# A fused attention and feed-forward block: four early copies placed on other engines

## The chip, the cores and the metric

The kernel runs on one core of a Trainium2 chip. A core has a matrix engine (TensorE, PE in the profile, with its weight loads listed apart as PEld), three engines for elementwise work (VectorE or DVE, ScalarE or ACT, GpSimd or POOL), and SyncE (SP), which here only issues DMAs. Each engine works through its own list of instructions in order; between engines the order is kept by semaphores. The metric is the device time of one execution in microseconds (us). Several runs are given by their median, lowest and highest.

## The reference

All inputs are bfloat16. S is 2048 tokens, D 448, H 16 heads of Dh 28, the attention window W 256, F 1792.

```python
xn = _layernorm(x, axis=-1)                       # (x - mean) / sqrt(var + 1e-5)
return x + _A_ref(xn, A_wqkv, A_wo) + _B_ref(xn, B_w_gate, B_w_up, B_w_down)
...
qkv = (lambda x, *d: x.transpose(*d))((x @ wqkv).reshape(B, S, 3, H, Dh), 2, 0, 3, 1, 4)
scores = jnp.einsum("bhqd,bhkd->bhqk", q, k) * (Dh ** -0.5)
mask = (idx[:, None] - idx[None, :] >= 0) & (idx[:, None] - idx[None, :] < W)
scores = jnp.where(mask[None, None], scores, -1e9)
p = _softmax(scores, axis=-1)
o = jnp.einsum("bhqk,bhkd->bhqd", p, v)           # then @ wo
...
return (_gelu(x @ w_gate) * (x @ w_up)) @ w_down  # B
```

Both branches read the same normalized rows; their sum and x give the output.

## The kernel before

The 2048 rows are 16 tiles of 128. Four tiles make a block of 512 query columns (`qb` 0 to 3). A block runs through attention (scores, exponentials, masks, products with v) and then through the gated feed-forward; while the scores of a block are at work, matmuls of other stages are fed in between by a planner with costs in ns (`Feed`, `share`). The change lies ahead of all this, in the straight prologue of lines 674 to 720, which is written out by hand: each engine's list is in the order of the calls there. The prologue normalizes the first four tiles, turns them and makes the q, k and v of the first block for the first group of four heads.

One tile `t` goes through these steps. `stat(t)` (lines 195 and 196, DVE) takes mean and variance of 448 columns. `rstd(t)` (lines 200 and 201, ACT) makes 1/sqrt as exp of a logarithm. `norm(t)` (line 209) writes `xn`, 512 columns: 448 normalized ones by DVE (the main part), and then the last 64 a second time into columns 448 to 511 (the doubled columns). The doubling exists because 448 is three and a half times 128: the fourth chunk of 128 rows holds the same 64 rows twice, so that two half-height matmuls can use both halves of the array. For tiles 1, 2, 5, 6 and 7 the doubled columns are written by POOL, for all others by DVE. `xn` has four buffers. `transp(t)` (lines 223 and 224) turns the four chunks on PE into PSUM, chunk 3 being the one with the doubled columns, and one engine copies the result to `xnT`. `v_dense` and `proj` (line 228) are the three full chunks of a projection, `v_half` and `qk_halves` (line 234) the half-height rest.

The weights also need a layout of their own. Heads of 28 are padded to 32 columns, so `pads` (line 665) copies raw q or k columns from `wraw` to `wqp` or `wkp`, group by group of four heads, and line 692 does the same for the last 64 weight rows of q and of k, into `w3p`: on partitions 0 to 63 those of q, on 64 to 127 those of k. `proj(pq, wqp, 0, 0)` needs the first group of `wqp`, the `proj` for k needs `wkp`, and `qk_halves` needs `w3p`. After `norm(3)` comes `make_masks` on POOL: one memset of 768 columns (line 155) and 18 small selects (line 161).

SP issues the loads of x and the weights in the order of the listing. ACT issues those of x tile 1 and of the first q and k columns ahead of its own work. None of these issues is in the part that changes.

Of the kernel before, what the change touches and what calls it, by code (L numbers as in the profile page):

```python
# [15 lines left out]
S, D, H, Dh, F = 2048, 448, 16, 28, 1792  # L16
# [59 lines left out]
def kernel(  # L76
# [11 lines left out]
    nc = tc.nc  # L88
# [25 lines left out]
    wraw = blk.tile([P, 4, 2 * D], bf16, name="wraw", tag="hT")  # L114
# [54 lines left out]
    wqp = const.tile([P, 3, H, 32], bf16, name="wqp")  # L169
    wkp = const.tile([P, 3, H, 32], bf16, name="wkp")  # L170
    w3p = const.tile([P, H, 32], bf16, name="w3p")
# [33 lines left out]
    def norm(t):  # L205
        xn = work.tile([P, 4, P], bf16, name="xn", bufs=4)
        xf = xn[:, :, :].rearrange("p a b -> p (a b)")
        for eng, lo, n, src in ((nc.vector, 0, D, 0), (nc.gpsimd if t in (1, 2, 5, 6, 7) else nc.vector, D, 64, 384)):
            eng.tensor_scalar(out=xf[:, lo:lo + n], in0=x_sb[:, t, src:src + n], scalar1=mv_all[:, t, 0:1],
                              scalar2=rstd_all[:, t:t + 1], op0=ALU.subtract, op1=ALU.mult)  # L210
        xns[t] = xn
# [5 lines left out]
    def transp(t, n, copy, tag):  # L217

        tp = psum.tile([P, 2, 4, P], bf16, name="tp", tag=tag, bufs=2 if tag == "m" else 1)
        for i in range(n):  # L220
            xn = xns.pop(t + i)
            for c in range(4):
                nc.tensor.transpose(out=tp[:, i, c, :], in_=xn[:, c, :], identity=ident[:, :])
        copy(out=xnT[:, :, t * P:(t + n) * P].rearrange("p c (i q) -> p i c q", q=P), in_=tp[:, 0:n, :, :])
# [15 lines left out]
    def bank(name):  # L240

        tag = ring[0][ring[1] % len(ring[0])]
        ring[1] += 1
        return psum.tile([P, QB], f32, name=name, tag=tag, bufs=2 if tag == "m" else 1)


    def v_dense(t, pv):
        mm3(pv, lambda c: xnT[:, c, t * P:(t + 1) * P], lambda c: wv[:, c, :], True, False)
# [411 lines left out]
    def pads(eng, dst, gs):  # L660

        hs = slice(4 * gs.start, 4 * gs.stop)
        c0 = D * (dst is wkp)
        src = wraw[:, 0:3, c0 + Dh * hs.start:c0 + Dh * hs.stop]
        eng(out=dst[:, :, hs, 0:Dh], in_=src.rearrange("p c (h d) -> p c h d", d=Dh))
# [11 lines left out]
    stat(1)  # L677
    rstd(1, 1)
    norm(0)
    transp(0, 1, nc.scalar.copy, "o")  # L680
    stat(2)
    norm(1)
    rstd(2, 1)
    warmup(1)
# [3 lines left out]
    pvs = [bank("pv")[:, 0:D]]  # L688
    v_dense(0, pvs[0])
    norm(2)  # L690
    pads(nc.vector.tensor_copy, wqp, slice(0, 1))
    nc.vector.tensor_copy(out=w3p[:, :, 0:Dh], in_=wraw[:, 3, 0:D].rearrange("p (h d) -> p h d", d=Dh))
    pads(nc.scalar.copy, wkp, slice(0, 1))
    transp(2, 1, nc.scalar.copy, "o")
    pvs.append(bank("pv")[:, 0:D])
    v_dense(1, pvs[1])
    norm(3)
# [246 lines left out]
```

## Time and profile before

| | us |
|---|---|
| median of 3 runs | 221.85 |
| lowest, highest | 221.24, 221.89 |
| the profiled execution's own time | 221.75 |
| its span, first to last instruction | 220.0 |
| outside the span | 1.75 |
| PE busy in the span | 213.2 (97%) |
| DVE, ACT, POOL busy | 153.1, 133.3, 48.0 |

The table holds one profiled execution beside three unprofiled ones. All times inside the span are counted from its first instruction. In the timeline view a line gives the start, the duration, the engine, the line of the kernel, the operation, its output and inputs with their shapes, the count (several instructions of one kind are merged, and the duration is then that of the whole stretch), and in brackets how long the engine was idle before and what ended that. [...] In the view of the chain that ended last a line has a start, a length, an engine, an output and a line of the kernel. The PE is busy without a gap from 20 to 60 us; the prologue is the stretch up to about 12 us.

### The profile page before, as it was taken

The numbers are of one execution on the slowest core, as the hardware profiler recorded it, in microseconds if no ns is written. First come the engines' busy times: TensorE is split into PE (matmuls) and PEld (weight loads), VectorE is DVE, ScalarE is ACT, GpSimd is POOL, SyncE is SP. The second block draws the span as 40 slices with busy tenths as digits, with TensorE's granted clock in tenths as the row PEclk, the third lists the DMA queues.
The fourth block names the chain that finished last, engine by engine and source line by source line (L and its number), as shares of the span: only waits on it lengthen the run. The fifth ranks groups of instructions, "written<-read, shape, count | busy, mean of one in ns | idle before, by whom it ended". The sixth has DMA issues, their size and how long they took to land.

```text
span 220.0 us, 5437 instructions
## 1 busy us (share of the span) xinstructions
PE 213.2 (97%) x2281; PEld 95.8 (44%) x2281; DVE 153.1 (70%) x346; ACT 133.3 (61%) x131; POOL 48.0 (22%) x81
## 2 busy tenths in 40 slices
PE   6999999999999999999999999999999999999992
PEld 2433333444444454444444445444344445434571
DVE  5987896799666883669566795385345898579422
ACT  3588788662878875432878887233576777574000
POOL 5767987320000220022000021022000022022000
PEclk9999999999999999999999999999999999999999
DMA  6996799203200001101400000200000000000010
GB/s 188 308 293 89 188 316 289 56 1 75 45 3 21 24 24 28 19 11 38 71 1 24 24 0 24 53 12 0 0 3 21 25 3 24 24 1 0 22 46 25
DMA packets 18045, 13.30 MB, mean 60 GB/s; under 512 B 8704, under 2 KB 16992, under 8 KB 18016
## 3 DMA queue, kind: packets, MB, share of 16 engines
q1 hardware_dynamic: 17072, 12.62, 22.3%
q8 instruction: 19, 0.31, 0.6%
q10 hardware_dynamic: 944, 0.29, 0.5%
q14 instruction: 10, 0.08, 0.1%
HBM read 9.15 MB, written 2.18 MB: 51 GB/s over the span
## 4 chain that ended last, share of the span: by engine, by line
PE 93%; DVE 3%; DMA 1%; ACT 1%; issue 0%; DVEq 0%
PE po L376 20%; PE gt L228 16%; PE u L228 12%; PE sc L611 6%; PE po L371 6%; PE gt L234 5%; PE ue L228 5%; PE ov L571 5%; PE pq L228 4%; PE pv L228 4%; PE pk L228 3%; PE pq L234 1%; PE g L228 1%; DMA x_sb<-in_A_x_dram 1%; PE ue L234 1%; PE pv L234 1%
## 5 line engine op out<-in xcount | busy, mean ns | idle before, releaser
L617 ACT ACTIVATE p_sb<-sc 128x2048 bf16<-128x2048 f32 (+2 forms) x42 | 73.8, 1757 | 12.6 <-PE sc L611 8.2
L376 PE MATMUL po<-wd,hT 128*128 128x448 bf16 (+1 forms) x238 | 49.8, 342 | 0.0
L459 ACT ACTIVATE ge<-gt 128x1024 bf16<-128x1024 f32 x26 | 26.6, 1024 | 34.9 <-PE u L234 20.1
L537 POOL TENSOR_TENSOR oN<-oc,l 128x512 bf16<-128x512 f32 x12 | 16.0, 1332 | 137.8 <-DVE l L551 87.4
L228 PE MATMUL gt<-xnT,wg 128*128 128x512 bf16 x156 | 37.5, 380 | 0.0
L466 DVE TENSOR_TENSOR hT<-ge,u 128x512 bf16<-128x512 bf16 x40 | 25.7, 682 | 12.9 <-ACT ge L459 12.9
L376 PEld LDWEIGHTS <-hT 128*128 128x128 bf16 x238 | 21.5, 98 | 18.8 <-issue 2.6
L228 PE MATMUL u<-xnT,wu 128*128 128x512 bf16 x120 | 29.2, 379 | 0.0
L518 DVE TENSOR_TENSOR p_sb<-p_sb,masks 128x256 bf16<-128x256 bf16 (+1 forms) x90 | 26.8, 352 | 0.4 <-ACT p_sb L617 0.4
L228 PEld LDWEIGHTS <-wg 128*128 128x128 bf16 x168 | 15.3, 98 | 21.3 <-issue 4.5
L228 PEld LDWEIGHTS <-wu 128*128 128x128 bf16 x168 | 16.0, 98 | 19.2 <-issue 1.0
L556 DVE TENSOR_TENSOR oc<-oc,ov 128x512 f32<-128x512 f32 x12 | 8.2, 686 | 16.5 <-ACT oc L555 16.5
L611 PE MATMUL sc<-qT,kT 28*64 28x320 bf16 (+7 forms) x640 | 16.9, 263 | 0.2
L410 DVE CAST hT<-ue 128x512 bf16<-128x512 f32 x16 | 10.2, 681 | 8.3 <-PE ue L234 8.3
L371 PE MATMUL po<-wo,oN 128*128 128x448 bf16 (+1 forms) x68 | 15.9, 343 | 0.0
L381 DVE TENSOR_TENSOR res<-po,x_sb 128x448 bf16<-128x448 f32 (+1 forms) x17 | 9.9, 585 | 8.6 <-PE po L376 8.4
L528 POOL TENSOR_SCALAR_AFFINE_SELECT p_sb<-p_sb 128x512 bf16<-128x512 bf16 (+1 forms) x20 | 14.2, 729 | 5.4 <-ACT p_sb L617 5.4
L234 PE MATMUL gt<-xnT,wgu 64*128 64x512 bf16 (+1 forms) x67 | 12.7, 380 | 0.0
L555 ACT COPY oc<-ov 128x512 f32<-128x512 f32 x12 | 7.0, 583 | 8.8 <-PE ov L571 8.8
L228 PE MATMUL pq<-xnT,wqp 128*128 128x512 bf16 x45 | 12.2, 380 | 0.1
L543 DVE STREAM_TRANSPOSE l<-oc 128x512 f32<-128x512 f32 x16 | 11.3, 703 | 1.4 <-POOL oN L537 1.2
L228 PE MATMUL ue<-xnT,wu 128*128 128x512 bf16 x48 | 12.0, 380 | 0.0
(92 smaller groups left out, 243.4 us busy)
## 6 DMA issues: line engine op xcount, KB each, us to landing
out_dram<-res SPq DMA_DIRECT2D x15, 112.0 KB
x_sb<-in_A_x_dram SPq DMA_DIRECT2D x3, 448.0 KB
wu<-in_B_w_up_dram SPq DMA_DIRECT2D x1, 1344.0 KB
wg<-in_B_w_gate_dram SPq DMA_DIRECT2D x1, 1344.0 KB
wd<-in_B_w_down_dram SPq DMA_DIRECT2D x3, 448.0 KB
wraw<-in_A_wqkv_dram SPq DMA_DIRECT2D x2, 252.0 KB
wo<-in_A_wo_dram SPq DMA_DIRECT2D x4, 98.0 KB
wv<-in_A_wqkv_dram SPq DMA_DIRECT2D x1, 336.0 KB
```

The lines of the kernel that those rows point to most:

```text
L228: nc.tensor.matmul(ps, lhsT=lhs(c), rhs=rhs(c), start=start and c == 0, stop=stop and c == 2, skip_group_check=True)
L234: nc.tensor.matmul(ps[c:c + m], lhsT=lhs[p0:p0 + 64, c:c + m], rhs=rhs[p0:p0 + 64], start=start, stop=stop, tile_position=(p0, c), skip_gr ...
L371: nc.tensor.matmul(po[:, 0:w], lhsT=oN[:, g, cs], rhs=wo[:, g, lo:up], start=(g == 0), stop=False, skip_group_check=True)
L376: nc.tensor.matmul(po[:, 0:w], lhsT=hT[:, f, cs], rhs=wd[:, f, lo:up], start=False, stop=(f == NF - 1), skip_group_check=True)
L459: nc.scalar.activation(out=ge[:, :, :], in_=pr["gt"][:, :, :], func=ACT.Gelu_apprx_tanh)
L466: nc.vector.tensor_tensor(out=hT[:, f + i, :], in0=ge[:, i, :], in1=u, op=ALU.mult)
L518: nc.vector.tensor_tensor(out=reg, in0=reg, in1=m, op=ALU.mult)
L528: nc.gpsimd.affine_select(out=reg, in_=reg, pattern=mid + [[1 if diag else -1, min(w, P)]], compare_op=ALU.is_ge, fill=0.0, base=0 if diag ...
L537: nc.gpsimd.tensor_tensor(out=oN[:, g, :], in0=oc[:, :], in1=inv, op=ALU.mult)
L543: nc.vector.transpose(out=l1[:, :, :].rearrange("p a b -> p (a b)"), in_=oc[:, :])
L611: nc.tensor.matmul(ss[k0:k0 + nk, j, col:col + nq], lhsT=kT[r, g, kt * P + k0:kt * P + k0 + nk], rhs=qT[r, g, qb * QB + q0:qb * QB + q0 + ...
L617: nc.scalar.activation(out=p_sb[:, :, 0:ncol], in_=ss[:, :, 0:ncol], func=ACT.Exp, scale=SCALE)
```

## The change

Four pieces of work move to another place; nothing is computed in another way. The doubled columns of tile 0 go from DVE to POOL. The first group of `wqp` is copied by ACT and not by DVE, and the copy of `w3p` by POOL and not by DVE. On ACT, the copy of tile 2's turned chunks out of PSUM now comes ahead of the two padding copies.

```diff
     def norm(t):
         xn = work.tile([P, 4, P], bf16, name="xn", bufs=4)
         xf = xn[:, :, :].rearrange("p a b -> p (a b)")
-        for eng, lo, n, src in ((nc.vector, 0, D, 0), (nc.gpsimd if t in (1, 2, 5, 6, 7) else nc.vector, D, 64, 384)):
+        for eng, lo, n, src in ((nc.vector, 0, D, 0), (nc.gpsimd if t in (0, 1, 2, 5, 6, 7) else nc.vector, D, 64, 384)):
...
     pvs = [bank("pv")[:, 0:D]]
     v_dense(0, pvs[0])
     norm(2)
-    pads(nc.vector.tensor_copy, wqp, slice(0, 1))
-    nc.vector.tensor_copy(out=w3p[:, :, 0:Dh], in_=wraw[:, 3, 0:D].rearrange("p (h d) -> p h d", d=Dh))
-    pads(nc.scalar.copy, wkp, slice(0, 1))
     transp(2, 1, nc.scalar.copy, "o")
+    for dst in (wqp, wkp):
+        pads(nc.scalar.copy, dst, slice(0, 1))
+    nc.gpsimd.tensor_copy(out=w3p[:, :, 0:Dh], in_=wraw[:, 3, 0:D].rearrange("p (h d) -> p h d", d=Dh))
     pvs.append(bank("pv")[:, 0:D])
     v_dense(1, pvs[1])
     norm(3)
```

The lists of PE and SP keep their order. DVE's list loses three instructions. ACT's list gains the `wqp` copy and has, after the logarithm and exponential of tile 3, the copy of tile 2, then `wqp`, then `wkp`. POOL's list has, after its two opening memsets of `v_sb` (lines 142 and 143), the doubled columns of tiles 0, 1 and 2, then `w3p`, then the masks. Three waits are new: chunk 3 of tile 0 on PE waits for POOL, the weight loads of the first q projection wait for ACT and those of `w3p` for POOL; and `norm(4)` on DVE, which writes the `xn` buffer that tile 0 had, now also waits for POOL.

## The prediction

> **What bounds the kernel.** I read the page first: the shares of the engines and the chain that ended last.
>
> ```profile
> PE 213.2 (97%) x2281; PEld 95.8 (44%) x2281; DVE 153.1 (70%) x346; ACT 133.3 (61%) x131; POOL 48.0 (22%) x81
> ...
> PE 93%; DVE 3%; DMA 1%; ACT 1%; issue 0%; DVEq 0%
> ```
>
> 93% of the chain is PE. The change touches no matmul, so it can only move the moment from which PE has work without a break; later stages move along with it. The 3% of DVE lie in the prologue, as the chain of 4 to 14 us shows:
>
> ```profile
> 7.51 0.31 DVE wqp L665
> 7.82 0.87 DVE w3p L692
> 8.69 0.32 DVE xn L209
> 9.01 0.05 issue
> 9.05 0.44 PE tp L223 x4
> 9.49 0.57 PE pv L228 x3
> 10.06 1.40 PE s L228 x6
> ```
>
> Two of the copies that leave DVE are on it, ahead of tile 3's normalization. So the gain cannot be the 0.31 + 0.87 by itself: it is what tile 3's chain wins until its next limit. For that, the timelines of DVE, POOL and ACT, 7 to 9.7 us:
>
> ```profile
> 7.23 0.36 DVE L209 TENSOR_SCALAR xn<-x_sb,mv_all,rstd_all 128x448 bf16<-128x448 bf16 x1
> 7.51 0.31 DVE L665 COPY wqp<-wraw 128x336 bf16<-128x336 bf16 x1
> 7.74 0.94 DVE L692 COPY w3p<-wraw 128x448 bf16<-128x448 bf16 x1
> 8.61 0.60 DVE L209 TENSOR_SCALAR xn<-x_sb,mv_all,rstd_all 128x448 bf16<-128x448 bf16 x2
> 9.53 0.42 DVE L224 COPY xnT<-tp 128x512 bf16<-128x512 bf16 x1 [0.33 <-PE tp L223]
> ```
>
> ```profile
> 7.21 0.68 POOL L209 TENSOR_SCALAR xn<-x_sb,mv_all,rstd_all 128x64 bf16<-128x64 bf16 x1 [0.92 <-ACT rstd_all L201]
> 7.82 0.73 POOL L155 MEMSET masks<- 128x768 bf16 x1
> 8.63 1.29 POOL L161 TENSOR_SCALAR_AFFINE_SELECT masks<-masks 64x64 bf16<-64x64 bf16 x5
> ```
>
> ```profile
> 7.27 0.58 ACT L224 COPY xnT<-tp 128x512 bf16<-128x512 bf16 x1 [0.16 <-PE tp L223]
> 7.75 0.30 ACT L200 ACTIVATE lnv<-mv_all,eps_t 128x1 f32<-128x1 f32 x1
> 8.08 0.20 ACT L201 ACTIVATE rstd_all<-lnv 128x1 f32<-128x1 f32 x1
> 8.19 0.45 ACT L665 COPY wkp<-wraw 128x336 bf16<-128x336 bf16 x1
> 8.55 0.58 ACT L224 COPY xnT<-tp 128x512 bf16<-128x512 bf16 x1
> ```
>
> To see: the exponential that gives tile 3's scale ends at 8.28, DVE starts tile 3 at 8.61 only because the w3p copy is in front. That copy took 0.94 for 448 columns, where the wqp copy of 336 took 0.31; it lies beside POOL's memset of the masks.
>
> **The change, part by part.**
>
> *Tile 0's doubled columns, DVE to POOL.* DVE starts its next work 0.21 earlier (5.24 to 5.45). POOL is idle from 3.64 and starts 0.11 after the scale, as it did for tile 1 (5.60 to 5.71): 4.87 + 0.11 = 4.98. Its five such instructions last 0.57 to 0.68, so it ends at 5.55 to 5.66, against 5.54 on DVE. Chunk 3 of tile 0 is late by 0 to 0.1; I take 0.05, the mean of the ends. ACT's copy of tile 0 (6.09), tile 2's logarithm and exponential (6.58, 6.91) follow it: tile 2's scale comes at 7.16, not 7.11. POOL's pad of tile 1 starts at 5.71 as before.
>
> *What the 0.21 is worth.* Statistics of tile 2 and the main part of tile 1 are 0.21 earlier, so tile 1's chunks are turned at about 6.4 and not 6.62. ACT's copy of tile 1 waited 0.16 for that and now waits for ACT's own exponential of tile 2: about 7.07, not 7.27. Logarithm and exponential of tile 3 follow: its scale at 8.08, not 8.28. Tile 2 gains nothing: its scale is 0.05 later, and so are POOL's pad (7.94) and chunk 3 of its turn.
>
> *The two copies off DVE.* Tile 3 now starts when its scale is there: 8.08 + 0.09 = 8.17 instead of 8.61. Undisturbed, its two parts (0.60) are done at 8.77 instead of 9.21.
>
> *ACT's order.* The copy of tile 2 no longer waits for wkp: it starts when tile 2 is turned, 8.33 + 0.02 = 8.35, and ends at 8.93 instead of 9.13. wqp then takes 8.83 to 9.28 and wkp 9.19 to 9.64 (0.45 each by the wkp row). They are needed by the q projection (10.01 before) and the k projection (10.65 before): hidden. If tile 3 were 0.7 earlier still, wqp would be next.
>
> *PE.* The v matmuls of tile 1 end issuing at 8.73; tile 3's first chunks can go then (before: 9.05), chunk 3 at 8.94, v of tile 2 at 9.01 (its copy is there at 8.93), DVE's copy of tile 3 at 9.21 and the q projection at 9.69 instead of 10.01. Sum if POOL disturbs nothing: **-0.32**.
>
> *w3p on POOL.* It starts behind tile 2's pad, at 7.87. POOL copies no such shape before. Lower bound: its small copies (line 321, 48 columns, 0.16 from start to start) and their slope against 16 columns (0.14) give 0.4; upper bound: the strided memset of v_sb, 768 columns, 1.53. Nearest in size is the select of 512 columns, 0.63; I take 0.55. It is needed at 11.39 by the half-height matmuls: it would have to last 3 us to be late. Behind it the masks end at 14.1 (15.1 at the bound) instead of 13.57; POOL's next work started at 15.11, on an exponential of ACT. Hidden.
>
> *What tile 3 meets on DVE.* The memset of the masks goes from 7.82 to about 8.42, beside tile 3. The only row that shows a DVE copy beside that memset is w3p itself: 0.94, and 0.31 + 112 columns at the 0.35 ns that the larger pads show would be 0.35; so 0.59 was lost to it. Bounds of what it costs tile 3: nothing (main parts at 7.23, 17.36 and 18.36, beside POOL's pads and selects, keep 0.36), or 0.59. The memset falls behind the main part (8.17 to 8.53) and ahead of the doubled columns (8.45), as it fell behind wqp and ahead of w3p; by that nearest row I take 0.4 to 0.59 on the doubled columns. They end at about 9.3, and the q projection is at 10.1: -0.32 + 0.4 (the PE slack is used first) gives **+0.1**.
>
> [...]
>
> *New waits.* norm(4) at 14.04 waits on POOL for tile 0's pad, done at about 5.6: nothing; behind it would be DVE's v and kT casts and the transposing DMA of tile 4 on SP. The DMA queues get no new work, and no DMA wait stands in this stretch behind 3.47, so the loads hide nothing here.
>
> The sum is against the profiled 221.75 (220.0 + 1.75), which is 0.10 under the median: 221.75 + 0.1 = **221.85**. A measurement of this kernel tells about 0.3% (0.67) from no change.
>
> **The rivals.**
>
> 1. *Undisturbed tile 3.* The memset costs DVE nothing: -0.32, 221.4. For it: the three unlengthened main parts. Against: the w3p row.
> 2. *Both parts of tile 3 blocked.* POOL's w3p copy also holds DVE's main part, from 8.17 to the copy's end (8.42), and the memset then takes its 0.59: tile 3 ends at 9.6, and the cost is 9.6 - 9.21 = +0.4, 222.15. For it: the same w3p row; against: 17.36. [...]
> 3. *Slower: the clock step of PE moves.* The first v product of 448 columns is followed after 0.38, the next after 0.35, the third after 0.19: PE runs at half rate until about 7.75, and the eight warm-up matmuls before took 0.45 each, not 0.215. The work from 7.75 to the end of the q and k projections at 11.3 is seven v products, eight turns and six projections: 7 x 0.19 + 8 x 0.065 + 6 x 0.215 = 3.1 us. At half rate each us of later step costs up to 0.9; some slack (0.3) goes first. A step late by 1.7 costs about 1.2, 222.95; from about 1.1 on it is over 0.3%. For it: tile 0's chunk 3 now waits for POOL, and the spread of the runs, 0.65, fits a step that wanders. Against: PE's other gaps get smaller. [...]
> 4. *Faster by more.* -0.32, and the step comes earlier by the 0.35 that the first two v products lose: -0.7, 221.05. Against: tile 2's turn waits for POOL's pad at 7.94, whatever PE's rate.
>
> **How the numbers follow.** Forecast (doubled columns blocked, +0.1): 0.36. Rival 1: 0.24, of which 0.05 end under -0.3% by the spread of the runs. Rival 2: 0.12, of which 0.04 end over +0.3%. Rival 3: 0.17. Rival 4: 0.11. Faster: 0.05 + 0.11 = 0.16; slower: 0.04 + 0.17 = 0.21; within: 0.63. The range goes from 221.1 (rival 4 mostly left out) to 222.9 (the dearer half of rival 3 left out). The likeliest case's own range, from the bounds of the block, is 221.5 to 222.2.
>
> **What would show it.** Right: ACT's copy of tile 2 ahead of 8.4, tile 3's main part at about 8.2, its doubled columns ending at 9.1 to 9.4, the q projection at 9.9 to 10.2, w3p on POOL under 0.8, and the same PE busy time after 20 us. Doubled columns at 8.8 would be rival 1, a main part of 0.6 rival 2; v products of 0.35 after 8 us rival 3. I would be wrong with a wait that I count as hidden (w3p at 11.4, the masks at 15.1), or if a shift of some tenths changes the order in which exponentials and matmuls meet in the first block, where DVE is busy 4.91 of 5 us from 15 to 20.

## The result, and the profile after

| | median, us | lowest to highest | runs |
|---|---|---|---|
| before | 221.50 | 221.12 to 221.89 | 22 |
| after | 221.81 | 221.43 to 222.29 | 22 |

The changed kernel takes 1.0017 times as long, with a 95% interval of 1.0011 to 1.0023: slower by about 0.4 us (0.3 by the medians). The three runs that the prediction started from have a median of 221.85; more runs of the same kernel put it at 221.50. So the predicted 221.85 lies next to the measured 221.81, but the predicted step (+0.1, no change) does not: there is a loss, clear of the noise. That the two levels agree is luck: the profiled 221.75 from which the sum started is 0.25 over the median of before, and this made up for a loss that was taken 0.2 to 0.3 too small.

The profiled execution after took 221.50, with a span of 219.8. It is 0.31 under its median, and the first profile of before is 0.25 over its own; the spans of the two, 219.8 and 220.0, therefore stand the wrong way round. The stages do not mislead. The chain that ended last of the changed kernel, 4 to 14 us, around tile 3 (start, length, engine, output, line):

```profile
7.56 0.21 ACT rstd_all L201
7.77 0.03 issue
7.80 1.21 DVE xn L209
9.01 0.04 issue
9.06 0.45 PE tp L223 x4
9.51 0.57 PE pv L228 x3
10.07 1.40 PE s L228 x6
```

The w3p copy is gone from the chain, and in its place the normalization of tile 3 itself has grown from 0.32 to 1.21. From the timelines of DVE, POOL and ACT of the changed kernel, 7.2 to 9.7 us, the rows around tile 3:

```profile
7.80 1.42 DVE L209 TENSOR_SCALAR xn<-x_sb,mv_all,rstd_all 128x448 bf16<-128x448 bf16 x2 [0.51 <-ACT rstd_all L201]
```

```profile
6.96 0.70 POOL L209 TENSOR_SCALAR xn<-x_sb,mv_all,rstd_all 128x64 bf16<-128x64 bf16 x1 [0.84 <-ACT rstd_all L201]
7.64 0.56 POOL L694 COPY w3p<-wraw 128x448 bf16<-128x448 bf16 x1
8.13 0.74 POOL L155 MEMSET masks<- 128x768 bf16 x1
```

```profile
7.56 0.20 ACT L201 ACTIVATE rstd_all<-lnv 128x1 f32<-128x1 f32 x1
7.98 0.59 ACT L224 COPY xnT<-tp 128x512 bf16<-128x512 bf16 x1 [0.22 <-PE tp L223]
8.46 0.47 ACT L665 COPY wqp<-wraw 128x336 bf16<-128x336 bf16 x1
8.84 0.47 ACT L665 COPY wkp<-wraw 128x336 bf16<-128x336 bf16 x1
```

In the records neighbouring instructions of one engine overlap, on ACT here by 0.11 and 0.09 (8.57 and 8.46, 8.93 and 8.84). Everything on ACT went as planned: the scale of tile 3 is ready at 7.76, tile 2's copy starts at 7.98, both weight copies are done by 9.31. DVE even waits 0.51 for the scale. Then the two instructions of tile 3 last 1.42; the same two of tile 4, at 14.04 in the profile before and with POOL idle, took 0.59. The main part alone, in a narrow window of the same timeline:

```profile
7.80 1.20 DVE L209 TENSOR_SCALAR xn<-x_sb,mv_all,rstd_all 128x448 bf16<-128x448 bf16 x1 [0.51 <-ACT rstd_all L201]
```

It ends at 9.00, and POOL's copy and memset end at 8.87. PE pays for it. In its timeline

```profile
7.78 0.73 PE L228 MATMUL pv<-wv,xnT 128*128 128x448 bf16 x3
9.06 0.45 PE L223 MATMUL tp<-ident,xn 128*128 128x128 bf16 x4 [0.54 <-DVE xn L209]
```

PE waits 0.54 for tile 3, where it waited 0.16 before. From 20 us on PE is busy without a gap as before, so what was lost by the q projection stays lost.

### The profile page after: what moved, and what is told of

Read it like the earlier page. It is cut to its first block, busy times and chain, and to the rows that moved or that the text cites. A ratio compares the mean times of both kernels' runs of the same rounds, so it can differ in the third digit from the quotient of the medians.

```text
span 219.8 us, 5439 instructions
## 1 busy us (share of the span) xinstructions
PE 212.4 (97%) x2281; PEld 95.4 (43%) x2281; DVE 152.7 (69%) x343; ACT 133.7 (61%) x132; POOL 49.5 (23%) x83
## 4 chain that ended last, share of the span: by engine, by line
PE 95%; DVE 2%; ACT 2%; issue 0%; DVEq 0%
PE po L376 20%; PE gt L228 16%; PE u L228 12%; PE sc L611 6%; PE po L371 6%; PE gt L234 5%; PE ue L228 5%; PE ov L571 5%; PE pq L228 4%; PE pv L228 4%; PE pk L228 3%; PE wps L190 2%; PE pq L234 1%; PE g L228 1%; PE ue L234 1%; PE pv L234 1%
```

## The experiments

The theory after the result: DVE's normalization cannot run while POOL is at its copy or its memset, and the change put both, back to back, on the moment when tile 3's scale arrives. Rivals: the weights come too late from ACT and POOL (or PE's new waits cost); the move of tile 0's columns costs.

**The memset of the masks out of the way.** The changed kernel with

```diff
+    nc.gpsimd.memset(masks[:, :, :, :], 1.0)
     def make_masks():
-        nc.gpsimd.memset(masks[:, :, :, :], 1.0)
```

> The changed kernel with the masks' memset moved ahead of POOL's first doubled columns, into POOL's idle time after the v_sb memsets. Theory (tile 3's main part on DVE is shut out while POOL works through w3p and the memset, 7.64 to 8.87): only the w3p copy, 7.64 to 8.20, is left; the main part lasts 0.65 to 0.7 and not 1.20, tile 3 ends at 8.7 and not 9.22, the q projection is at about 9.5 and not 10.02; 0.5 us less than the changed kernel, so about 0.1 less than before (ratio 0.9994). Rival (what costs is that the q weights and w3p come later from ACT and POOL, or the new waits on PE): the memset's place makes no difference, ratio 1.0017 as for the changed kernel, main part still 1.2.

Measured: 0.9987 of before (0.9978 to 0.9996), median 221.36. The timelines of its POOL and its DVE, 7.2 to 9.2 us:

```profile
7.85 0.55 POOL L694 COPY w3p<-wraw 128x448 bf16<-128x448 bf16 x1
8.37 0.86 POOL L161 TENSOR_SCALAR_AFFINE_SELECT masks<-masks 64x64 bf16<-64x64 bf16 x3
```

```profile
8.17 0.61 DVE L209 TENSOR_SCALAR xn<-x_sb,mv_all,rstd_all 128x448 bf16<-128x448 bf16 x2 [0.63 <-ACT rstd_all L201]
```

The two parts of tile 3 are back at 0.61 and the q projection at 9.60. The weights come from the same engines, at the same place in their lists: the rival of late weights falls. One detail is off: the main part starts inside the copy and lasts 0.40 (8.17 to 8.57), hardly more than its 0.36, where 0.65 to 0.7 was expected. Why one copy alone need not show is worked out under "What tile 3 meets on DVE" below.

**The copy out of the way.** The changed kernel with

```diff
-    nc.gpsimd.tensor_copy(out=w3p[:, :, 0:Dh], in_=...)
+    nc.scalar.copy(out=w3p[:, :, 0:Dh], in_=...)
```

> The changed kernel with the w3p copy on ACT, behind wkp, in place of POOL. Theory (POOL's work shuts DVE out): the memset now starts at 7.64 behind tile 2's doubled columns and ends at 8.38, the main part of tile 3 starts at 7.80 and lasts about 0.85, tile 3 ends at 8.9, the q projection is at about 9.65; 0.35 us less than the changed kernel, equal to before (ratio 1.000). ACT's w3p copy of about 0.6 ends at 9.9, in time for 11.4. Rival (late weights): w3p is now later by 1.7 us, so it would be no better than the changed kernel, 1.0017 or over.

Measured: 0.9997 (0.9988 to 1.0006), median 221.30. The main part starts at 7.98 and lasts 0.67 beside the memset (7.79 to 8.52), less than the 0.85 expected from a start at 7.80; the q projection is at 9.67, and w3p, which now lands at 9.96 and not 8.20, is missed by nobody.

**Both.**

> Both edits: the masks' memset early and w3p on ACT, so that POOL does nothing but selects beside tile 3. Theory: main part 0.36 to 0.4, tile 3 ends at 8.4, then PE and ACT's copy of tile 2 (8.57) limit: q projection at 9.3 to 9.4; 0.65 us less than the changed kernel, 0.28 less than before (ratio 0.9987), about the 0.32 of the prediction's undisturbed case. If the selects shut DVE out as well, the main part stays over 0.6 and the gain is half of that. Rival (late weights): 1.0017 or over.

Measured: 0.9993 (0.9984 to 1.0002), median 221.34: less than the expected 0.9987, which lies in the interval. The profile has the expected block-free tile 3, but the q projection at 9.57 and not at 9.3 to 9.4: x came 0.14 later than in the profile that I worked from, and PE came to its full rate late (the first three v products last 1.20, the next three 0.73). The timelines of POOL and DVE, 7.8 to 9.2 us, show the selects beside tile 3:

```profile
7.86 1.57 POOL L161 TENSOR_SCALAR_AFFINE_SELECT masks<-masks 64x64 bf16<-64x64 bf16 x6
```

```profile
8.13 0.61 DVE L209 TENSOR_SCALAR xn<-x_sb,mv_all,rstd_all 128x448 bf16<-128x448 bf16 x2 [0.59 <-ACT rstd_all L201]
```

Three of these six selects run beside tile 3 (from 8.14 to 8.94) and cost it nothing that can be seen. This does not yet show that a select leaves DVE alone: each lasts 0.23 to 0.24, too short to lengthen a main part that waits for it (worked out below).

**Tile 0's doubled columns back on DVE.**

```diff
-... (nc.gpsimd if t in (0, 1, 2, 5, 6, 7) else nc.vector, D, 64, 384) ...
+... (nc.gpsimd if t in (1, 2, 5, 6, 7) else nc.vector, D, 64, 384) ...
```

> The changed kernel with the doubled columns of tile 0 back on DVE; the other moves stay. Theory: tile 3's scale comes 0.2 later (about 8.0), but the end of its main part is set by POOL's memset (8.87), which hangs on tile 2's scale and not on this; so the time stays, ratio 1.0015 to 1.002, main part about 1.0. Rival (the doubled columns of tile 0 on POOL, and PE's new wait for them, are what costs): back to before, 1.000.

Measured: 1.0016 (1.0007 to 1.0025). The loss stays without this part of the change, so it is not its cause. The main part starts at 8.15 and lasts 0.94: it starts later, and ends 0.13 after the memset (9.09 and 8.96), as in the changed kernel (9.00 and 8.87).

**The same two moves on the kernel before.** First the memset early, as above, with nothing else.

> The kernel before with only the masks' memset moved into POOL's idle time ahead of tile 1's doubled columns. Theory: DVE's w3p copy, 0.94 in the profile before, lasts 0.35 to 0.45 once no memset runs beside it; tile 3 then starts when its scale is there, at about 8.37 and not 8.61, and the q projection 0.24 earlier; ratio 0.9989. Rival (the w3p copy is slow by its shape): copy still 0.9, ratio 1.000.

Measured: 0.9987 (0.9978 to 0.9996), median 221.20. The w3p copy on DVE lasts 0.26: its 0.94 before was not its shape.

Then only the doubled columns of tile 0 to POOL.

> The kernel before with only the doubled columns of tile 0 on POOL. Theory: DVE is 0.2 ahead, so its w3p copy starts at about 7.55, ahead of the memset (7.87), and is not held up (0.35 to 0.5); but then tile 3's main part starts at about 8.2 inside the memset and lasts 0.6 to 0.7; q projection 0.1 to 0.15 earlier than before, ratio 0.9993 to 1.000. Rival (this move is what costs, by PE's new wait): slower than before, 1.001 or over.

Measured: 0.9999 (0.999 to 1.0008), so this part alone does nothing that can be measured. In its profile the w3p copy goes ahead of the memset (7.65, 0.26), and the memset falls on tile 3 instead (main part 0.72). What DVE wins in front, it waits for behind.

**The suspected waits doubled.** The changed kernel with the memset of the masks issued twice:

```diff
-        nc.gpsimd.memset(masks[:, :, :, :], 1.0)
+        nc.gpsimd.memset(masks[:, :, :, :], 1.0); nc.gpsimd.memset(masks[:, :, :, :], 1.0)
```

> The changed kernel with the masks' memset issued twice in a row. Theory (while POOL has such work queued back to back, DVE does not get in): tile 3's main part lasts 2.0 and not 1.20, the q projection is 0.8 later, ratio 1.005. If DVE gets a turn between two POOL instructions: main part 1.2 as it is, the doubled columns behind the second memset, q projection 0.6 later, ratio 1.0045. Rival (the weights come late): POOL's masks are 0.8 later with nothing waiting for them, ratio 1.0017.

Measured: 1.0036 (1.0022 to 1.005), median 222.26, q projection at 10.58. POOL, and the two parts of tile 3 on DVE in narrow windows:

```profile
7.71 0.55 POOL L694 COPY w3p<-wraw 128x448 bf16<-128x448 bf16 x1
8.21 1.54 POOL L155 MEMSET masks<- 128x768 bf16 x2
```

```profile
7.90 1.17 DVE L209 TENSOR_SCALAR xn<-x_sb,mv_all,rstd_all 128x448 bf16<-128x448 bf16 x1 [0.51 <-ACT rstd_all L201]
8.99 0.79 DVE L209 TENSOR_SCALAR xn<-x_sb,mv_all,rstd_all 128x64 bf16<-128x64 bf16 x1
```

The second of my two cases: the main part waits for the copy and the first memset, gets its turn between the memsets, and the doubled columns (0.29 alone) wait for the second. A longer POOL queue costs more, with nothing else touched.

And the copy issued twice, with the memset early:

```diff
-    nc.gpsimd.tensor_copy(out=w3p[:, :, 0:Dh], in_=...)
+    nc.gpsimd.tensor_copy(out=w3p[:, :, 0:Dh], in_=...); nc.gpsimd.tensor_copy(out=w3p[:, :, 0:Dh], in_=...)
```

> The changed kernel with the memset early (which gave 0.9987) and the w3p copy on POOL issued twice. There the main part of tile 3 started at 8.17 inside the single copy (7.85 to 8.37) and was not lengthened. If a POOL copy shuts DVE out as the memset does: the two parts of tile 3 last 1.0 to 1.2 and not 0.61, the q projection is 0.4 to 0.5 later, ratio 1.001. If only the memset does: 0.61 again, ratio 0.9987.

Measured: 1.0001 (0.9992 to 1.001). The second copy shows on the doubled columns (DVE, narrow windows):

```profile
8.13 0.41 DVE L209 TENSOR_SCALAR xn<-x_sb,mv_all,rstd_all 128x448 bf16<-128x448 bf16 x1 [0.59 <-ACT rstd_all L201]
8.46 0.60 DVE L209 TENSOR_SCALAR xn<-x_sb,mv_all,rstd_all 128x64 bf16<-128x64 bf16 x1
```

0.60 and not 0.29: a POOL copy holds DVE up as well, by 0.3 and not by the 0.4 to 0.6 that I expected of it, because the main part slipped in between the two copies: it ends at 8.54, 0.13 after the first copy (8.41), and the second starts at 8.47 (both estimated from POOL's merged row, two copies in 1.17 from 7.86, at 0.55 to 0.56 each).

**How much is one execution.** Both kernels were profiled again, unchanged.

> The kernel before, unchanged, profiled once more. Its first profile (221.75) is 0.25 over its median of 22 runs, and its q projection at 10.01 is later than the other kernels' times lead to expect: time less q start is 211.6 to 211.8 in all of them, and 211.5 there. Theory (a near tie): w3p on DVE (7.74) and the memset on POOL (7.82) race, and the first profile shows the rarer outcome; here w3p lasts 0.26 and tile 3's two parts, beside the memset, 0.9 to 1.0, q projection at 9.75 to 9.85. Rival (the first profile is typical): w3p 0.94 again, q projection at 10.0, and some 0.2 us of the changed kernel's loss arises behind the q projection.

> As the run above, a third look at the same kernel: w3p 0.26 and q projection at 9.75 to 9.85 by the near tie; 0.94 and 10.0 by the rival.

> The changed kernel once more. POOL's w3p copy and memset run back to back across the moment at which tile 3's scale comes, so there is no tie: main part 1.1 to 1.25 again, q projection at 10.0 to 10.2, whenever x arrives. If the main part came out under 0.7 here, the block would be a matter of the single execution, and the cause would be open.

The kernel before has three different pictures. In the first profile the memset falls on w3p. In the second it falls on tile 3 (DVE, 7.2 to 9.2 us):

```profile
7.65 0.28 DVE L692 COPY w3p<-wraw 128x448 bf16<-128x448 bf16 x1
8.15 0.87 DVE L209 TENSOR_SCALAR xn<-x_sb,mv_all,rstd_all 128x448 bf16<-128x448 bf16 x2 [0.21 <-ACT rstd_all L201]
```

In the third it starts earlier and falls on wqp and w3p together:

```profile
7.59 0.89 DVE L665 COPY wqp<-wraw 128x336 bf16<-128x336 bf16 x1
7.78 0.82 DVE L692 COPY w3p<-wraw 128x448 bf16<-128x448 bf16 x1
8.52 0.59 DVE L209 TENSOR_SCALAR xn<-x_sb,mv_all,rstd_all 128x448 bf16<-128x448 bf16 x2
```

So the near tie is there, but neither of my outcomes for it was the rule: the third profile shows one that I had not listed. What differs ahead of the three pictures is when x arrives (3.47, 3.30 and 3.55, DVE's first work on it) and how fast PE is by then: its last warm-up matmul takes 0.63, 0.63 and 0.38. The changed kernel repeats itself, for x 0.3 later:

```profile
8.11 1.17 DVE L209 TENSOR_SCALAR xn<-x_sb,mv_all,rstd_all 128x448 bf16<-128x448 bf16 x1 [0.51 <-ACT rstd_all L201]
```

All of them together. "Scale to end" goes from the end of ACT's exponential for tile 3 to the end of tile 3's second part on DVE. The ratio of each experiment is to runs of before that were taken beside it (medians 221.45 and 221.47), so it is not the quotient of two medians of the table:

| kernel | scale to end, us | q projection at | median, us | ratio |
|---|---|---|---|---|
| before, three profiles | 0.93, 0.91, 0.96 | 10.01, 9.82, 9.92 | 221.50 | 1 |
| after, two profiles | 1.46, 1.42 | 10.02, 10.29 | 221.81 | 1.0017 |
| after, memset early | 0.65 | 9.60 | 221.36 | 0.9987 |
| after, w3p on ACT | 0.91 | 9.67 | 221.30 | 0.9997 |
| after, both | 0.65 | 9.57 | 221.34 | 0.9993 |
| after, tile 0 back | 1.19 | 10.11 | 221.82 | 1.0016 |
| before, memset early | 0.65 | 9.59 | 221.20 | 0.9987 |
| before, tile 0 moved | 0.98 | 9.80 | 221.47 | 0.9999 |
| after, memset twice | 1.92 | 10.58 | 222.26 | 1.0036 |
| after, memset early, w3p twice | 0.96 | 9.87 | 221.51 | 1.0001 |

The median less the q projection's start is 211.6 to 211.8 in all rows with one profile: time moves one for one with that start. (The medians are those of all runs, the starts those of one execution. Within the profiled executions the span less the start is 209.8 to 210.2, so a single pair is good to some tenths and no better.) The mean start of before is 9.92 and of after 10.16, 0.24 apart; the medians differ by 0.31. The rest is inside what single profiles scatter.

## Why the prediction was wrong

*What bounds the kernel, and where the change acts.* Right: only the moment at which PE can go on without a break counts, and that moment is set by tile 3's chain.

*Tile 0 and ACT's order.* Right. The doubled columns of tile 0 lasted 0.71 on POOL against the assumed 0.57 to 0.68, tile 3's scale came with DVE waiting for it, tile 2's copy no longer waits for wkp, and wqp and wkp on ACT (0.47 each) were ready before their use. The case without disturbance, -0.32, fits what the kernels with an undisturbed tile 3 gave: 0.9987 (-0.29) with the memset early and 0.9993 (-0.16) with both edits, with intervals that reach from -0.5 to 0.

*w3p on POOL.* The size was right (0.56 against 0.55) and so was that nobody waits for its result. What I counted as hidden was the instruction's effect on DVE, which I had only as a rival.

*What tile 3 meets on DVE.* This is the step that failed. I took the block from the memset alone, on the doubled columns alone, 0.4 to 0.59, with the main part running free from 8.17. On the chip the main part itself, which comes 0.16 to 0.20 after the copy starts, waits for the copy and then for the memset behind it: 1.20 and 1.17 against 0.36, a block of 0.8. Rival 2 had this mechanism and the price +0.4; the measured ratio gives 0.38. I gave it 0.12, since the rows in which a main part keeps 0.36 beside POOL are rows beside selects and beside the 64-column pads, and I let them speak for the copy too. The doubled copy shows that they could not.

Those rows could not even speak for the selects. In eight profiles the main part of tile 3 ends 0.12 to 0.14 after the end of the POOL instruction that it waits for (9.00 and 8.87 in the first profile after, 8.65 and 8.52 with w3p on ACT, 9.07 and 8.94 with the memset twice, this 8.94 estimated from the start at 8.21 and 0.73). Where no wait shows it lasts 0.36 to 0.40. So a main part that starts within about 0.25 of that end (an estimate, 0.36 to 0.40 less 0.13) looks free, whether it waits or not. The main part at 17.36 lies beside POOL work from 16.96 to 18.22, which I read as one select. It is two, as narrow windows of POOL's timeline before show:

```profile
16.96 0.63 POOL L528 TENSOR_SCALAR_AFFINE_SELECT p_sb<-p_sb 128x512 bf16<-128x512 bf16 x1 [0.17 <-ACT p_sb L617]
17.55 0.67 POOL L528 TENSOR_SCALAR_AFFINE_SELECT p_sb<-p_sb 128x512 bf16<-128x512 bf16 x1
```

The first ends at 17.59, and the main part beside it (17.36 to 17.73) ends 0.14 later, where a waiting one would end too. The row at 18.36 lasts 0.40, and the doubled columns behind it, beside the rest of POOL's pad, 0.39 against 0.29. The single copy of the first experiment is the same case: it ends at 8.40, 0.23 after the main part's start.

For memset and copy the runs show that DVE is held up (0.26 became 0.94 beside the memset, 0.29 became 0.60 beside the second copy). For the selects they leave it open. Both parts of tile 3 take 0.61 beside them, and took 0.59 for tile 4 with POOL idle; but in two runs it is the selects that take longer: the first three 0.86 with the memset early on the changed kernel, against 0.80 in the first profiles of before and after, and the first eight 2.17 with it early on the kernel before, against 2.06 and 2.07. If one select takes all of it, that one lasts 0.29 and 0.34 in place of 0.23 (an estimate from these sums).

*The baseline.* The second error is that the term for before came from one profile in which the memset happened to fall on w3p, and in which the q projection was 0.1 later than in the mean of three. Before, DVE has two copies and tile 3 in the stretch, and the one memset falls on whichever is there; the cost is 0.3 of scale-to-end in each of the three pictures (0.91 to 0.96 against 0.65). The change takes away what DVE had in front of tile 3, and adds a second instruction of the kind that blocks: 1.42 to 1.46. Counted from DVE's first work on x, tile 3's scale comes 0.14 to 0.35 earlier (4.46 in both profiles after, 4.60 to 4.81 before), and scale to end is 0.5 longer: a sum of +0.15 to +0.36, with the measured 0.3 to 0.4 at its upper end. The upper end is also the nearer comparison: PE turns tile 1 in 0.40 in both profiles after and in the one of before with 4.60, but in 0.61 in the two with 4.81, so by that comparison only about 0.14 of the gain in front belongs to the change (0.20 was predicted).

*The rivals.* The step in PE's rate did move: in the first profile after, the first three v products take 0.73 together instead of 1.08, so the step came earlier there. It moves between executions of the kernel before too (1.08, 0.73 and 0.73), and is not what separates the two kernels. That it is a step of the clock was my reading: the granted clock is 1.00 in every stretch from 4 to 9 us in the first profiles of both. No run shows a step late by 1.7, the term behind rival 3's 222.95 and the upper end of the range, nor that a wait of PE delays it; in all thirteen profiles the first three v products take 0.73 to 1.21, so at most 0.5 was lost there (1.21 less 0.73). No projection waited for wqp, wkp or w3p. In the first profile after, PE waits 0.27 for the load of the v weights (6.96); this is ahead of tile 3, and the second profile, without it, has nearly the same scale to end (1.42 against 1.46).

What stays open: why the main part does not get in between the copy and the memset (1.17 to 1.20 in three profiles, and 0.94 with tile 0 back, where it starts later), when it does get in between two memsets and between two copies. In the records the memset starts 0.05 to 0.07 before the copy ends (8.13 and 8.20 in the first profile after), while a second memset or second copy starts about 0.06 after the first one's end (an estimate from the merged rows: two memsets in 1.54 at 0.73 to 0.74 each, two copies in 1.17 at 0.55 to 0.56 each). Whether that gap lets DVE in, or DVE makes the gap, no run shows. The experiments give the order, not the rule behind it.

## What to carry to other kernels

Work that is moved to an idle engine is not free if that engine can shut out another (here 0.36 on DVE became 1.20 beside POOL): look at which instruction of the other engine will stand beside it, and when, not only at whether its result is due. The sign here was an instruction that lasted some three times as long as its like (a copy 0.94 against 0.26, a normalization 1.20 against 0.36), and the wait stood in its bar, not in an idle gap. Before a row counts as evidence against a wait, check that a wait could have shown in it: beside a short instruction it could not, and a merged row can hide where one instruction ends. A memset that nobody waits for belongs where both engines are free: moved there, it gave 0.9987 on the kernel before and after alike.

## What the runs showed of the hardware

A POOL memset of 768 columns and a POOL copy of 448 held up DVE copies and tensor-scalar instructions on bfloat16 data: a copy of 448 columns lasted 0.26 to 0.28 undisturbed and 0.82 to 0.94 beside the memset; a normalization of 448 columns 0.36 to 0.40 where no wait shows, 0.65 to 0.72 beside the memset, and 0.94 to 1.20 beside the copy with the memset behind it; one of 64 columns 0.29 undisturbed and 0.60 beside a second copy. The wait lengthened the DVE instruction's bar and showed as no idle time (the idle 0.51 ahead of the 1.20 ended with ACT's scale). In eight profiles a normalization that waited ended 0.12 to 0.14 after the POOL instruction. Selects of 64 columns cost DVE nothing that could be seen (0.61 for two instructions beside them, 0.59 with POOL idle), but at 0.23 to 0.24 each they are too short to show it; in two runs they took longer themselves beside a normalization (three in 0.86 against 0.80, eight in 2.17 against 2.06). DVE got its turn between two memsets (its 64 columns started at 8.99, after a main part of 1.17), and between two copies (a main part of 0.41, then 0.60), but not between a copy and the memset behind it (1.17 to 1.20 in three profiles), where POOL's two records overlap by 0.05 to 0.07. PE was slower at first: in the first profile before, its v products follow one another after 0.38 and 0.35, and the next work follows the third after 0.19. The point at which it speeds up differed between executions of one kernel: the last warm-up matmul, at 5.7 to 5.9, lasted 0.63 in two profiles of the kernel before and 0.38 in the third.
